# Moving the eight weight sums of the last batch from VectorE to GpSimd

## The chip, the cores and the metric

The program runs on one core of one Trainium2 chip. A core has five engines with a queue of instructions each: TensorE (PE, with its weight loads shown as PEld), VectorE (DVE), ScalarE (ACT), GpSimd (POOL) and SyncE (SP, which here issues the DMAs of inputs, outputs and transposes). An engine takes its instructions in the order in which they stand in its queue; a semaphore holds an instruction until what it needs is there. The metric is the device time of one execution in microseconds. The number of a kernel is the median of its runs.

## The reference

Two layers follow each other, with four batches of 768 rows, 8 heads of 64 columns, 512 columns in all. The first is a recurrent attention with a decay for each head; the second mixes the rows and columns by a Fourier transform, normalizes, and puts two matrix products with a ReLU between them on top:

```python
for t in range(S):
    state = gamma * state + einsum(k[:, :, t], v[:, :, t])
    y[:, :, t] = scale * einsum(q[:, :, t], state)
x = y with the heads side by side                 # 4 x 768 x 512
u = x + real(fft(fft(x, axis=1), axis=2))
un = (u - mean(u)) / sqrt(var(u) + 1e-06)         # per row
out = u + maximum(un @ w_ch1, 0.0) @ w_ch2        # w_ch1 512 x 2048, w_ch2 2048 x 512
```

## The kernel before, in words

**Stages.** Each batch goes through the same stages. The heads come in pairs, four pairs to a batch. `cast_unit` (L417) turns a pair's q, k and v into f16 on GpSimd. `t_unit` has q and k transposed. `a_unit` (L657) makes the products of queries and keys on TensorE in three parts, and VectorE multiplies each part by a mask into the tile `atm` (L668). `kv_unit` (L674) makes the running states. `y_unit` (L700) adds up a pair's output on TensorE, from the states (L715) and from `atm` (L719), and ScalarE writes it to `x` (L727). `fold_s` (L744), `fold_d` (L771) and `fold_e` (L785, L787) add and subtract halves of `x` on VectorE, all in f16 with both inputs in SBUF, which shortens the Fourier products that follow (`s1_unit` L848, `s2_unit` L1010). `s2_unit` ends with two additions of `x` on GpSimd (L1038, L1040). `norm_unit` makes the statistics (L1050, L1051) and the normalized rows `un` (L1052), which are transposed into `unT`. Then come the two products of the channel layer.

**The channel layer.** In the first three batches `h_unit` (L1088, evicted by ScalarE L1092 or VectorE L1094) makes the hidden rows and `ch_unit` (L1127, L1131) the output rows. In the last batch, number 3, the second product goes through a seven-product scheme for 2 x 2 blocks. The rows come in three groups of 256. For each group `hp_unit` (L1175) makes the hidden blocks, evicted by ScalarE (L1180) and in one half by VectorE (L1183), VectorE adds some of them up (L1193), and `p_unit` (L1217) makes the seven products; VectorE adds each to where it belongs (L1222). Four of the products have sums of blocks of the second weight `w216` on their right side. These are the tiles `wsum`. `wsum_unit` (L1152) makes them: for k of 1 to 4 and for two parts, one subtraction of 128 x 1024 f16 elements each, so eight instructions. The sums for k = 2 and k = 4 take the sums for k = 1 and k = 2 as their second input. The eight tiles come from the pool `inp`, of 11 buffers, which also holds the loaded q, k and v.

**The order of the work.** The function `tile_retnet_recurrent__then__fnet_fourier_mix_kernel` collects units of work in streams. A stream has a first and a last due time, in units of one batch, and its units are spread evenly between them. `emit` (L1373) sorts all units by due time; that gives the order in the program. The framework then puts each engine's instructions in the order of its queue: by the order in the program, but with what is ready ahead of what isn't, as its own estimate of durations has it, so an instruction can come out well ahead of its due time. Two helpers tie the order down: `pin`, for the first batch, and `held` (L148), which adds to every instruction of a unit an order-only edge to the instruction just ahead of it in the program on the same engine. `cast_unit` is `held` that way.

**Around the change.** The last `cast_unit` of batch 3 is due at about 2.30. The stream of `wsum_unit` runs from `b + WS[0]` to `b + WS[1]` with b = 3, so from 3.00 to 3.12, beside the first units of the last batch's channel layer, and it isn't `held`. The next instructions of GpSimd in the program after the last cast are those of `s2_unit` for batch 3, the first of them due at about 2.73.

Of the kernel before, what the change touches and what calls it, by code (L numbers as in the profile page):

```python
# [53 lines left out]
LD0, LD1 = (0.223, 0.312), (-0.370, 0.140)  # L54
HT0 = (0.666, 0.693, 0.632, 0.590)
NPE = 2
WS = (0.0, 0.12)
KD = (2, 3)
NT = 0.6
ACT_ROWS = ((2, 5, 6, 7, 8, 9, 10, 14), (0, 3, 6, 7, 9, 10, 11, 12, 14, 15))  # L60
# [3 lines left out]
def kernel(  # L64
# [9 lines left out]
    nc = tc.nc  # L74
# [29 lines left out]
    w216 = const.tile([P, NFB, DM], f16, tag="w216")  # L104
# [43 lines left out]
    def held(unit):  # L148
        def run():
            ins = tc.nc.cur_bb.bb.instructions  # L150
            n0 = len(ins)
            unit()
            for n in range(n0, len(ins)):
                m = n - 1
                while m >= 0 and ins[m].engine != ins[n].engine:
                    m -= 1
                if m >= 0:
                    tc.add_manual_dep(ins[n], ins[m].name,
                                      mybir.DependencyInfo(mybir.DependencyClass.NoSync,
                                                           mybir.DependencyReason.DATA),  # L160
                                      reason="casts in turn")
        return run
# [232 lines left out]
    for j in range(2):  # L395
# [6 lines left out]
        t = const.tile([P, 257], f32, tag=f"qn_{j}", name=f"qn_{j}", padded_shape=[P, 260])  # L402
# [463 lines left out]
    def g0_unit(b, parts=(0, 1, 2)):  # L866
        def run():
            for part in parts:
                (g0_a, g0_b, g0_c)[part](b)
        return run  # L870
# [185 lines left out]
    def rstd_unit(b, rt):  # L1056
        def run():
            stats = lb[b]["st"]
            if b == 0 and rt == 0:
                bn_unit(0)()  # L1060
            sl = slice(3 * rt, 3 * rt + 3)
            nc.scalar.activation(stats[:, sl, 2:3], stats[:, sl, 1:2], AF.Sqrt, bias=epsT,
                                 scale=1.0)
            nc.vector.reciprocal(out=stats[:, sl, 3:4], in_=stats[:, sl, 2:3])
        return run

    def unT_unit(b, kb):
        def run():
            un, unT = lb[b].pop(("un", kb)), lb[b]["unT"]
            if b > 1 or b and kb >= 3:  # L1070
                nc.sync.dma_start_transpose(unT[:, :, kb * P:(kb + 1) * P], un)
                return
            pst = ps_g.tile([P, 4, P], f16, tag="g", name="pst", padded_shape=[P, 8, P])
            for cb in range(4):
                nc.tensor.transpose(pst[:, cb, :], un[:, cb * P:(cb + 1) * P], ident16)
            if (kb % 2 == 0) != (b == 0 and kb < 3):
                nc.vector.tensor_copy(unT[:, :, kb * P:(kb + 1) * P], pst)
            else:
                nc.scalar.copy(unT[:, :, kb * P:(kb + 1) * P], pst)
        return run  # L1080
# [61 lines left out]
    def spare(n, name):  # L1142
        return flat(inp.tile([P, 2, NCH, D], f32, tag="in32", name=name))[:, 0:n]
# [5 lines left out]
    def half_of(w, fh, eh, n0, n1):  # L1149
        return w[:, 8 * fh + n0:8 * fh + n1, 256 * eh:256 * eh + 256]  # L1150

    def wsum_unit(k, part):  # L1152


        def run():
            n0, n1 = 4 * part, 4 * part + 4
            t = seven["t", k, part] = spare(4 * 256, "wsum").rearrange("p (n m) -> p n m", n=4)
            a, b = {1: ((0, 1), (0, 0)), 2: ((1, 1), None), 3: ((1, 1), (0, 1)),
                    4: ((1, 0), None)}[k]
            in1 = half_of(w216, *b, n0, n1) if b else seven["t", k // 2, part]  # L1160
            nc.vector.tensor_tensor(out=t, in0=half_of(w216, *a, n0, n1), in1=in1,
                                    op=ALU.subtract)
        return run

    def hp_unit(b, g, n):

        def run():
            unT = lb[b]["unT"]
            if (g, n) == (0, 0):
                seven["s4"] = spare(8 * P, "s4").rearrange("p (n k) -> p n k", n=8)  # L1170
            psh = ps_pm.tile([P, 2, 256], f32, tag="pm", name="psh")
            for t in range(2):
                fb = n + 8 * t
                for cb in range(4):
                    nc.tensor.matmul(psh[:, t], w116[:, cb, fb * P:(fb + 1) * P],  # L1175
                                     unT[:, cb, g * 256:(g + 1) * 256],
                                     start=(cb == 0), stop=(cb == 3))
            for t0, t1, eng in (((0, 1, "a"), (1, 2, "v")) if n == 7 else ((0, 2, "a"),)):
                if eng == "a":
                    nc.scalar.activation(hg[:, n, t0:t1], psh[:, t0:t1], AF.Relu, bias=0.0,  # L1180
                                         scale=-1.0)
                else:
                    nc.vector.tensor_scalar(out=hg[:, n, t0:t1], in0=psh[:, t0:t1], scalar1=-1.0,  # L1183
                                            scalar2=0.0, op0=ALU.mult, op1=ALU.max)
            if n in (2, 5, 7):
                sl = slice({2: 0, 5: 3, 7: 6}[n], n + 1)
                a11, a12 = hg[:, sl, 0, 0:P], hg[:, sl, 1, 0:P]
                a21, a22 = hg[:, sl, 0, P:256], hg[:, sl, 1, P:256]
                s1, s2, s4 = sg[:, 0, sl], sg[:, 1, sl], seven["s4"][:, sl]
                for out_, x, y, op in ((s1, a21, a22, ALU.add), (s2, s1, a11, ALU.subtract),  # L1190
                                       (s4, a12, s2, ALU.subtract),
                                       (a21, a11, a21, ALU.subtract)):
                    nc.vector.tensor_tensor(out=out_, in0=x, in1=y, op=op)  # L1193
        return run
# [198 lines left out]
    streams = []  # L1393
    for b in range(B):
        majors = []
        if b == B - 1:
            for g in range(3):
                majors += [hp_unit(b, g, n) for n in range(8)]
                if g < 2:
                    majors.append(rstd_unit(b, g))  # L1400
                majors += [p_unit(b, g, k) for k in (1, 4, 5, 6, 2, 7, 3)]
            streams.append(([wsum_unit(k, part) for part in range(2) for k in (1, 2, 3, 4)],
                            b + WS[0], b + WS[1]))
        elif b == 0:
            for kb in range(3):
                if kb:
                    majors.append(unT_unit(0, kb))
                majors += [h0_unit(kb, g) for g in range(4)]
        else:
            majors += [h_unit(b, 0, fb) for fb in range(NFB)]  # L1410
        if b < B - 1:
            majors.append(rstd_unit(b, 0))
            majors += [ch_unit(b, 0, rb3, part) for rb3 in range(3) for part in range(4)]
            majors += [h_unit(b, 1, fb) for fb in range(NFB)]
            majors.append(rstd_unit(b, 1))
            majors += [ch_unit(b, 1, rb3, part) for rb3 in range(3) for part in range(4)]
        streams.append((majors, b, b + 1.0))
        streams += mix_units(b, [3, 4, 5], *(b + t for t in (DM0 if b == 0 else DM1)))
        if b + 1 < B:
            steps = attn_steps(b + 1)  # L1420
            if b == 0:
                streams.append(([load_unit(1, i, 6) for i in range(4)], LD0[0], LD0[1]))
                streams.append(([qt_zeros], 0.1, 0.15))
                streams.append(([half_tables], HT0[0], HT0[1]))
                streams.append(([pad_unit], HT0[2], HT0[3]))
                ts = TS0
            else:
                streams.append(([load_unit(b + 1, i) for i in range(4)], b + LD1[0], b + LD1[1]))
                n = [len(u) for u in steps[1:]]
                ts = list(TS1[:2]) + [TS1[2] + TS1[3] * sum(n[:j]) / sum(n) for j in range(6)]  # L1430
            streams.append((steps[0], b + ts[0], b + ts[1]))
            streams += [(u, b + ts[j + 2], b + ts[j + 3]) for j, u in enumerate(steps[1:])]
            end = b + ts[-1]
            da = DA0 if b == 0 else DA1
            sums = [s1_unit(b + 1, e, cb) for cb in range(2) for e in range(2)]
            sums.insert(1, g0_unit(b + 1, (1, 2)))
            streams.append((sums, end + da[0], end + da[1]))
            streams += mix_units(b + 1, [0, 1, 2], *(end + t for t in da[2:]))
# [31 lines left out]
```

## Time and profile before

| | |
|---|---|
| median of 3 runs | 242.05 us (241.75 to 242.3) |
| the profiled execution | 243.38 us, of which the span of its instructions is 240.6 us |
| granted TensorE clock | 0.999 |
| busy in the span | PE 226.1 us, DVE 189.6 us, ACT 125.2 us, POOL 82.0 us |
| the eight sums (L1161, DVE) | starts at 139.0, 140.4, 158.7, 159.5, 200.1, 201.1, 202.7 and 203.5 us |
| last batch's channel layer | first matmul at 194.63 us, last at about 237 us |

Times in the profile are microseconds from the span's start. A row of the time line gives the start, the duration from the first start to the last end of a run of like instructions, the engine, the line, the operation, output and inputs, shapes, and how many there are (x2: two, merged in one row); in square brackets stands how long the engine sat idle before it and what ended the wait. A row of a source line gives the least, the median and the greatest duration in ns. A row of a stretch gives its length and each engine's busy time in it. The chain of work that ended last is followed back from the last instruction, at each step to what released it.

### The profile page before, as it was taken

How to read it: one execution, taken by the hardware profiler on the slowest of the kernel's cores; microseconds unless marked ns; L12 is line 12 of the kernel's file. 1: busy time of each engine (PE TensorE's matmuls, PEld its weight loads, DVE VectorE, ACT ScalarE, POOL GpSimd, SP SyncE). 2: the span in 40 equal slices, each digit the busy share in tenths (PEclk: the TensorE clock that was granted, in tenths of full speed). 3: DMA queues.
4: the chain of work that ended last, by engine and by line, in shares of the span. 5: the costliest groups of instructions: out<-in, count | busy, mean ns of one | idle time of the engine just before them, and what ended most of it. 6: DMA issues, size and time to landing. Idle time of an engine off the chain costs nothing.

```text
span 240.6 us, 5573 instructions
## 1 busy us (share of the span) xinstructions
PE 226.1 (94%) x2127; PEld 154.8 (64%) x2127; DVE 189.6 (79%) x472; ACT 125.2 (52%) x272; POOL 82.0 (34%) x148
## 2 busy tenths in 40 slices
PE   0888999999999999999899999999999998899994
PEld 0366779756774656665567446655675477688883
DVE  8699987948898889977886759997886529968473
ACT  5989759675864544931147405822356336251430
POOL 7378802575300197850001817930003204200000
PEclk9999999999999999999999999999999999999999
DMA  7999999999999489979999587675100240140202
GB/s 169 236 269 260 207 207 207 217 245 247 243 232 213 78 193 217 186 142 123 256 277 210 112 177 203 131 120 159 44 3 0 70 131 0 40 115 1 90 0 87
DMA packets 101241, 36.78 MB, mean 153 GB/s; under 512 B 91488, under 2 KB 98528, under 8 KB 101216
## 3 DMA queue, kind: packets, MB, share of 16 engines
q1 hardware_dynamic: 96992, 32.25, 63.5%
q0 software_dynamic: 4224, 4.19, 10.6%
q8 instruction: 16, 0.26, 0.5%
q14 instruction: 9, 0.07, 0.1%
HBM read 27.26 MB, written 6.29 MB: 139 GB/s over the span
## 4 chain that ended last, share of the span: by engine, by line
PE 79%; DVE 7%; DMA 6%; POOL 2%; ACT 2%; issue 1%; SPq 1%; POOLq 0%; DVEq 0%
PE psc L1127 23%; PE psh L1088 21%; PE ps L1217 7%; PE psh L1175 6%; PE psh L1105 3%; PE wkA L665 3%; DMA qTz<-q16z 3%; DMA v<-in_v_dram 3%; PE ps L848 3%; PE wkY L719 2%; PE pq L1010 1%; PE ps L828 1%; PE wkY L715 1%; PE wkK L684 1%; SPq L217 1%
## 5 line engine op out<-in xcount | busy, mean ns | idle before, releaser
L1127 PE MATMUL psc<-w,ht 128*128 128x512 f16 x288 | 67.7, 379 | 0.0
L1088 PE MATMUL psh<-unT,w 128*128 128x384 f16 x320 | 59.5, 326 | 0.0
L1038 POOL TENSOR_TENSOR u<-u,x 128x256 f32<-128x256 f32 x21 | 13.8, 655 | 109.7 <-DVE u L1017 97.4
L1127 PEld LDWEIGHTS <-ht 128*128 128x128 f16 x288 | 27.2, 98 | 26.5
L1088 PEld LDWEIGHTS <-w 128*128 128x128 f16 x320 | 29.9, 98 | 15.9 <-DMA unT<-un 0.4
L1092 ACT ACTIVATE ht<-psh 128x384 f16<-128x384 f32 x46 | 22.3, 489 | 24.1 <-PE psh L1088 23.6
L668 DVE TENSOR_TENSOR atm<-wkA,maskp 128x512 f16<-128x512 f32 x36 | 23.6, 682 | 2.1 <-PE wkA L665 2.1
L1180 ACT ACTIVATE ht<-psh 128x512 f16<-128x512 f32 (+1 forms) x24 | 13.6, 569 | 19.3 <-PE psh L1175 17.1
L1052 ACT ACTIVATE un<-u,stats 128x512 f16<-128x512 f32 x21 | 14.7, 718 | 15.5 <-DVE stats L1051 9.0
L1175 PE MATMUL psh<-unT,w 128*128 128x256 f16 x192 | 22.6, 273 | 0.0
L1131 DVE SCALAR_TENSOR_TENSOR ob<-psc,stats,u 128x512 f32<-128x512 f32 x18 | 13.4, 744 | 9.9 <-PE psc L1127 9.7
L1094 DVE TENSOR_SCALAR ht<-psh 128x384 f16<-128x384 f32 x34 | 18.7, 550 | 2.7 <-PE psh L1088 2.5
L1175 PEld LDWEIGHTS <-w 128*128 128x128 f16 x192 | 18.6, 98 | 2.5 <-DMA unT<-un 0.2
L694 DVE SCALAR_TENSOR_TENSOR s<-s,gk,wkK 128x128 f16<-128x128 f16 x48 | 16.2, 337 | 2.3 <-ACT s L690 1.6
L727 ACT ACTIVATE x<-wkY,gexp 128x384 f16<-128x384 f32 x24 | 12.9, 580 | 9.0 <-PE wkY L719 8.9
L1050 DVE BATCH_NORM_STATS2 bst<-u 128x6 f32<-128x512 f32 x21 | 14.4, 687 | 3.2 <-POOL u L1040 2.8
L1217 PEld LDWEIGHTS <-ht 128*128 128x128 f16 x144 | 13.8, 98 | 4.1 <-ACT ht L1180 1.5
L439 POOL TENSOR_SCALAR kd<-k,gexp 128x384 f16<-128x384 f32 x24 | 13.8, 585 | 3.7 <-DMA k<-in_k_dram 3.6
L1193 DVE TENSOR_TENSOR ht<-ht 128x384 f16<-128x384 f16 (+1 forms) x27 | 9.2, 369 | 6.1 <-ACT ht L1180 5.9
L665 PE MATMUL wkA<-qTz,kT 128*128 128x256 f16 x72 | 13.2, 272 | 0.6 <-DMA qTz<-q16z 0.6
L1040 POOL TENSOR_TENSOR u<-u,x 128x256 f32<-128x256 f32 x21 | 13.4, 640 | 1.0 <-DVE u L1020 1.0
L1217 PE MATMUL ps<-wsum,ht 128*128 128x256 f16 x96 | 12.1, 273 | 0.4 <-DVE ht L1183 0.4
(190 smaller groups left out, 396.3 us busy)
## 6 DMA issues: line engine op xcount, KB each, us to landing
q<-in_q_dram SPq DMA_DIRECT2D x16, 384.0 KB, 5.9
k<-in_k_dram SPq DMA_DIRECT2D x16, 384.0 KB, 5.6
v<-in_v_dram SPq DMA_DIRECT2D x16, 384.0 KB, 5.9
out_dram<-ob SPq DMA_DIRECT2D x21, 256.0 KB, 2.7
w<-in_moe_w_ch_dram POOLq DMA_DIRECT2D x8, 512.0 KB, 10.7
out_dram<-ob SPq DMA_DIRECT2D x5, 128.0 KB, 2.0
unT<-un SPq DMA_TRANSPOSE x15, 2.5
kT<-kd SPq DMA_TRANSPOSE x10, 3.0
```

What stands on the lines that cost most here:

```text
L439: kc = nc.gpsimd.tensor_scalar(out=kd[:, :, h2, :], in0=k32[:, h2], scalar1=gkd[:, h0 + h2:h0 + h2 + 1], scalar2=1.0, op0=ALU.mult, op1=AL ...
L665: mm = nc.tensor.matmul(wk[:, c2], st["kT"][:, c, :], st["qT"][:, :, c, :], start=True, stop=True)
L668: nc.vector.tensor_tensor(out=st["atm"][:, 2 * part:2 * part + 2], in0=wk, in1=maskp[:, PAIR_ORDER[i]].unsqueeze(1).to_broadcast([P, 2, 2, ...
L694: nc.vector.scalar_tensor_tensor(out=s16[:, c], in0=s16[:, c - 1], scalar=gk2[:, hp:hp + 1], in1=wk[:, c - c0], op0=ALU.mult, op1=ALU.add)
L1050: nc.vector.bn_stats(bst, u[:, kb, :])
L1052: nc.scalar.activation(un, u[:, kb, :], AF.Identity, bias=stats[:, kb, 0:1], scale=-1.0)
L1088: nc.tensor.matmul(psh, w116[:, cb, fb * P:(fb + 1) * P], unT[:, cb, rt * 384:(rt + 1) * 384], start=(cb == 0), stop=(cb == 3))
L1092: nc.scalar.activation(ht16[:, fb, :], psh, AF.Relu, bias=0.0, scale=-1.0)
L1094: nc.vector.tensor_scalar(out=ht16[:, fb, :], in0=psh, scalar1=-1.0, scalar2=0.0, op0=ALU.mult, op1=ALU.max)
L1127: nc.tensor.matmul(psc, ht16[:, fb, rb3 * P:(rb3 + 1) * P], w216[:, fb, :], start=(fb == 0), stop=(fb == NFB - 1))
L1175: nc.tensor.matmul(psh[:, t], w116[:, cb, fb * P:(fb + 1) * P], unT[:, cb, g * 256:(g + 1) * 256], start=(cb == 0), stop=(cb == 3))
L1217: nc.tensor.matmul(ps[:, c0:c1], lhsT, rhs[:, c0:c1], start=bool(new and n == 0), stop=(n == 7), skip_group_check=True)
```

## The change

The eight subtractions of `wsum_unit` are issued on GpSimd in place of VectorE. Their due times go from 3.00 to 3.12 down to 2.42 to 2.60, behind the last casts of q, k and v, and each is `held`, so that GpSimd takes them in turn behind the last cast. What is subtracted from what, the tiles and their pool stay.

```diff
-WS = (0.0, 0.12)
+WS = (-0.58, -0.40)
...
             in1 = half_of(w216, *b, n0, n1) if b else seven["t", k // 2, part]
-            nc.vector.tensor_tensor(out=t, in0=half_of(w216, *a, n0, n1), in1=in1,
+            nc.gpsimd.tensor_tensor(out=t, in0=half_of(w216, *a, n0, n1), in1=in1,
                                     op=ALU.subtract)
...
-            streams.append(([wsum_unit(k, part) for part in range(2) for k in (1, 2, 3, 4)],
+            streams.append(([held(wsum_unit(k, part)) for part in range(2) for k in (1, 2, 3, 4)],
                             b + WS[0], b + WS[1]))
```

## The prediction

> **What bounds the kernel now.** I read first the busy time by stretch, to see where TensorE isn't full, then the chain that ended last for those places, then the time line of GpSimd and VectorE where the sums would go.
>
> ```profile
> 158.50:167.00 8.50, 8.50 (x86) 4.99 (x84) 6.95 (x16) 2.31 (x5) 0.01 (x1) 1.00 0.69 124
> 167.00:179.00 12.00, 12.00 (x103) 7.60 (x101) 11.12 (x25) 4.30 (x10) 0.00 (x0) 1.00 0.12 45
> 194.60:212.80 18.20, 16.54 (x154) 13.99 (x153) 15.11 (x38) 8.72 (x20) 4.28 (x6) 1.00 0.17 40
> 212.80:223.70 10.90, 10.90 (x102) 9.75 (x100) 8.11 (x22) 3.44 (x7) 0.00 (x0) 1.00 0.16 56
> ```
>
> The columns are the stretch, its length, and busy PE, PEld, DVE, ACT and POOL. TensorE is the bound: it is full in every row but the third, the last batch's first group, where it lacks 18.20 - 16.54 = 1.66 us. That is all that the change can win there. The second row is the one to remember: there VectorE is 11.12 of 12.00 us busy and TensorE has no gap either.
>
> ```profile
> 200.20 0.60 DVE wsum L1161
> 201.20 0.60 DVE wsum L1161
> 202.19 0.60 DVE bst L1050
> 203.54 0.58 DVE wsum L1161
> PE ps L1217 <- ACT ht L1180: 1.2, 1, 1.2
> PE ps L1217 <- DVE ht L1183: 0.4, 1, 0.4
> ```
>
> The chain runs through three of the sums (four rows of the chain, then two of the waits between 194 and 214 us). The statistics that they hold up hold up ScalarE, which comes late with the last hidden block; hence the 1.2 and 0.4 us in which TensorE waits.
>
> **What the change takes from VectorE.** Eight sums, of which four stand outside that group:
>
> ```profile
> 139.04 0.77 DVE L1161 TENSOR_TENSOR wsum<-w 128x1024 f16<-128x1024 f16 x1
> 143.13 0.75 DVE L1131 SCALAR_TENSOR_TENSOR ob<-psc,stats,u 128x512 f32<-128x512 f32 x1 [2.06 <-PE psc L1127]
> 158.68 0.66 DVE L1161 TENSOR_TENSOR wsum<-w 128x1024 f16<-128x1024 f16 x1
> 161.16 0.75 DVE L1131 SCALAR_TENSOR_TENSOR ob<-psc,stats,u 128x512 f32<-128x512 f32 x1 [0.32 <-PE psc L1127]
> ```
>
> The two near 139 us are followed by 2.06 us in which VectorE has nothing to do, the two near 159 us by 0.32 us, and TensorE is full there: nothing is won. The four in the first group take some 0.6 us each, 2.4 us of VectorE. Bounds: 1.66 us won if every wait of TensorE there goes, and half a microsecond lost if the new order of VectorE's queue happens to be worse. I take 1.4 won, since the two waits are near the sums (1.2 + 0.4) and small ones remain.
>
> **What it puts on GpSimd.** The time from the last cast to GpSimd's next work, and durations from which to price a sum:
>
> ```profile
> 157.67 0.83 POOL L444 TENSOR_SCALAR v<-v 128x768 f16<-128x768 f32 x1
> 183.25 0.63 POOL L1038 TENSOR_TENSOR u<-u,x 128x256 f32<-128x256 f32 x1 [24.74 <-DVE u L1017]
> L1038 POOL TENSOR_TENSOR u<-u,x x21: 632/635/1016, 40.4 to 204.9; 128x256 f32<-128x256 f32 x21
> L480 POOL TENSOR_SCALAR v<-v 128x768 f16<-128x768 f32 x2 | 1.7, 830 | 5.1 <-DMA v<-in_v_dram 5.1
> L480 POOL TENSOR_SCALAR v<-v 128x384 f16<-128x384 f32 x3 | 1.5, 501 | 0.5 <-DMA v<-in_v_dram 0.5
> ```
>
> The sums can start at 158.5, when the last cast ends. A cast of one input costs (830 - 501) / 384 = 0.857 ns an element and 0.17 us beside that. The two-input addition of 256 elements takes 0.635 us. With the same 0.17 us fixed, it costs 1.81 ns an element, and 1024 elements take 2.03 us. With nothing fixed they take four times 0.635, 2.54 us; with the rate of a cast and all the rest fixed, 1.29 us. I take 2.2 us, between the first two, since that row is the same operation. The Trainium skill (GPSIMD Engine Reference, section 3.1) gives 4497 ns for 2048 f32 elements; a line through that and our 635 ns gives an estimate of 2.29 us, by which the sum below would be some 0.6 us more. Eight sums are 17.6 us, to 176.1: well ahead of 183.25, where GpSimd's next work would queue behind them, and ahead of the products that need them (from 203 us). No DMA is issued or moved. Seen alone, that is free.
>
> **What they collide with.** VectorE's and GpSimd's instructions get in each other's way if VectorE's has two inputs in SBUF:
>
> ```profile
> 198.10 0.63 POOL L1038 TENSOR_TENSOR u<-u,x 128x256 f32<-128x256 f32 x1 [10.02 <-DVE u L1017]
> 198.69 0.75 POOL L1040 TENSOR_TENSOR u<-u,x 128x256 f32<-128x256 f32 x1
> 198.33 0.62 DVE L1193 TENSOR_TENSOR ht<-ht 128x384 f16<-128x384 f16 x1
> 198.33 1.33 DVE L1193 TENSOR_TENSOR ht<-ht 128x384 f16<-128x384 f16 x2
> L1193 DVE TENSOR_TENSOR s<-ht x9: 284/346/353, 199.9 to 233.1; 128x384 f16<-128x384 f16 x6, 128x256 f16<-128x256 f16 x3
> 17.24 1.17 POOL L368 TENSOR_SCALAR ssn<-ssp 128x1158 f16<-128x1158 f16 x1
> 17.81 0.80 DVE L761 TENSOR_TENSOR xab<-x 128x387 f16<-128x387 f16 x1
> L668 DVE TENSOR_TENSOR atm<-wkA,maskp x36: 656/681/692, 56.3 to 171.1; 128x512 f16<-128x512 f32 x36
> ```
>
> An L1193 addition takes 0.35 us alone. The one that starts at 198.33 under a GpSimd addition ends at 198.95, just behind GpSimd's end at 198.73. The next ends at 199.66, behind the end of the second GpSimd addition (199.44), which had come in between. So each waits for the whole instruction of the other, and they go in turn. The longest hold in this trace is at 17.24: an L761 that would take 0.35 us takes 0.80, until GpSimd's 1.17 us are over. An instruction with one input in PSUM doesn't wait: L668 keeps to 656 to 692 ns, casts beside it or not. No run yet shows a hold of 2.2 us. The Trainium skill (SBUF — State Buffer, "SBUF: two separate sides") says that the pair of ports which VectorE and GpSimd share is locked for the whole instruction, whatever its length; by that rule the price is the one below, and the trace agrees as far as its 1.17 us reach.
>
> Now what VectorE has to do while the sums run:
>
> ```profile
> 167.10 1.04 DVE L744 TENSOR_TENSOR xab<-x 128x780 f16<-128x780 f16 x2 [0.16 <-ACT x L727]
> 168.17 1.03 DVE L771 TENSOR_TENSOR eo<-xab 128x768 f16<-128x768 f16 x2
> 169.12 0.68 DVE L668 TENSOR_TENSOR atm<-wkA,maskp 128x512 f16<-128x512 f32 x1
> 170.53 1.28 DVE L668 TENSOR_TENSOR atm<-wkA,maskp 128x512 f16<-128x512 f32 x2
> 173.43 1.01 DVE L744 TENSOR_TENSOR xab<-x 128x768 f16<-128x768 f16 x2
> 171.69 0.59 PE L719 MATMUL wkY<-v,atm 128*128 128x64 f16 x12
> 172.11 6.10 PE L1088 MATMUL psh<-unT,w 128*128 128x384 f16 x36
> ```
>
> At 167.10 VectorE begins four folds in a row, L744 twice and L771 twice, all f16 with both inputs in SBUF. Sum 4 ends at 158.5 + 4 x 2.2 = 167.3, so the first fold waits 0.2 us. Sum 5 then goes ahead of the second fold, sum 6 ahead of the third, sum 7 ahead of the fourth: 3 x 2.2 = 6.6 us. VectorE is through at 169.1 + 6.8 = 175.9. Behind it in its queue stand the three L668 that make `atm`, and TensorE's L719 needs all three. Before, the last ends at 170.53 + 1.28 = 171.81 and L719 begins at 171.69: no slack. TensorE's queue is in order, so the 36 matmuls of L1088 wait behind L719: **TensorE stands for 6.8 us.** The last sum ends near 177.7, before the next pair of folds (173.43 + 6.8 = 180.2), so nothing more is held up. Bounds for a sum of 2.03 to 2.54 us: 6.8 to 8 us or so, by where in a sum the first fold falls; for 1.29 us, where seven are over when it arrives, some 1.7 us.
>
> **What the standing costs beyond itself.** Matmuls after a long idle time, and the same shape in mid-run:
>
> ```profile
> 5.61 0.82 PE L497 MATMUL tq<-ident,q16z 128*128 128x128 f16 x6 [5.61 <-POOL q16z L454]
> 8.13 1.91 PE L172 MATMUL wps<-ht 128*128 128x512 f16 x4
> 10.81 1.21 PE L172 MATMUL wps<-ht 128*128 128x512 f16 x3
> 164.48 1.03 PE L1127 MATMUL psc<-w,ht 128*128 128x512 f16 x4
> ```
>
> After 5.61 us idle at the program's start, four matmuls of 512 columns take 1.91 us, against 1.03 later: half the speed, though the granted clock is shown as full there. Three at 10.81 take 1.21 us, between 0.81 at full and 1.48 at half speed, so the speed came back near 11.4, some 3.3 us after the dense work began. If 6.8 us of standing have the same effect, TensorE loses half of 3.3 us: 1.7 us. Bounds: 0, since it may be a matter of the start alone, and 1.9 (half of the 3.8 us from 8.13 to the first full-speed work near 11.95). I take 1.7, as the idle times are alike. The Trainium skill (TensorE: Matmul & The Clock Gate, Part 1) says that an idle window of about 3.4 us halves the clock until about 3.4 us of sustained work; by that the price is 1.7 us as well, and no run here shows an idle time of that length in mid-run.
>
> **The sum**, against the profiled execution: 6.8 + 1.7 - 1.4 = 7.1 us on a span of 240.6 and a time of 243.38, so 250.5 for that one. The median of the runs is 242.05, 1.33 less; from it the prediction is 242.05 + 7.1 = **249.1 us**.
>
> **The rivals.** *The clock holds.* All as above without the 1.7: 247.4 us. For it: no mid-run case in the trace.
>
> *Short sums.* If GpSimd takes f16 faster, say 1.5 us a sum, five are over by 166.0 and the sixth ends at 167.5. The first fold waits 0.4, the next two 1.5 each: 3.4 - 1.4 = 2.0, so 244.0 us, with a standing too short to slow the clock. Against it: GpSimd's f16 instruction at 17.24 costs 1.17 us for 1158 elements, the rate of its f32 casts.
>
> *No collision, the change does what it says.* It wins its 1.4 us: 240.7 us, faster. It decides if the sums are over before the first fold, which takes under 8.6 / 8 = 1.08 us a sum, or if the folds come elsewhere in VectorE's new queue. Against it: the row of 0.635 us for a quarter of the elements, and that the folds at 167.10 start when ScalarE's L727 lets them, whatever the sums do.
>
> *GpSimd goes first each time.* If its next sum takes the ports before a waiting fold does, the first fold waits for all eight: 176.1 - 167.1 = 9.0, and 9.0 + 1.7 - 1.4 = 9.3, so 251.4 us. The turns at 198 us speak against it.
>
> **How the numbers follow.** Chances: forecast 0.46, the clock holds 0.20, short sums 0.12, GpSimd first 0.08, no collision 0.11, no change to be told 0.03. No change is within 0.2%, about what a measurement of this kernel can tell. The first four are slower: 0.86. The forecast alone lies in 248 to 251 us; the range from the short sums to GpSimd first, 243.6 to 251.6 us, leaves out 0.14.
>
> **What would show it.** In the changed profile, eight GpSimd subtractions from 158.5 on, near 2.2 us each, four of them longer by a few tenths; the folds L744 and L771 that follow them over 2 us each in place of 0.55; TensorE waiting for VectorE's L668 at L719 by some 7 us; then matmuls of 384 columns at twice their spacing for about 3 us; and between the start of the last channel layer and its second group nearly no wait of TensorE. It is wrong if the folds keep their 0.55 us under a running sum, if the sums are through by 167, or if the framework places the four folds or the sums elsewhere.

## The result, and the profile after

The changed kernel takes 250.11 us (median of 4 runs, 249.79 to 251.55). The kernel before, run beside it on the same chip, takes 242.18 us (4 runs, 241.75 to 243.01). The ratio is 1.0335, with a 95% interval of 1.0286 to 1.0384: slower by 3.4%, 7.9 us. The profiled execution took 250.03 us, its span is 248.3 us against 240.6, and its mean granted clock is 0.986.

The page's busy times of the changed kernel, and below them five stretches of it (columns as in the prediction: the stretch, its length, busy PE, PEld, DVE, ACT and POOL, granted clock, and what the DMA engines did):

```profile
PE 227.7 (92%) x2127; PEld 155.6 (63%) x2127; DVE 192.2 (77%) x464; ACT 125.4 (50%) x272; POOL 99.3 (40%) x156
```

```profile
167.00:179.00 12.00, 5.26 (x47) 3.21 (x45) 11.90 (x9) 0.64 (x2) 8.52 (x4) 0.81 0.08 29
202.60:220.80 18.20, 16.77 (x156) 14.30 (x155) 13.21 (x35) 8.80 (x20) 3.80 (x6) 1.00 0.19 51
...
174.00:175.00 1.00, 0.00 (x0) 0.00 (x0) 1.00 (x1) 0.00 (x0) 1.00 (x1) 0.70 0.00 0
175.00:176.00 1.00, 0.00 (x0) 0.00 (x0) 1.00 (x2) 0.00 (x0) 0.60 (x1) 0.50 0.00 0
181.00:182.00 1.00, 1.00 (x7) 0.53 (x5) 0.95 (x3) 0.43 (x1) 0.00 (x0) 0.88 0.00 0
```

The stretch from 167 to 179 us had TensorE busy for all of its 12.00 us; now it is busy for 5.26. VectorE looks as busy as ever (11.90 in place of 11.12), but with 9 instructions in place of 25: a blocked instruction counts as busy. That is why the busy share of the whole run doesn't show the trouble: VectorE's total went up by 2.6 us although eight instructions were taken from it. The last three rows are the granted clock around the standstill.

The time line of the same place in the changed kernel, for POOL, DVE and PE (start, duration, engine, line, what, and the idle time ahead of it):

```profile
157.84 2.13 POOL L1161 TENSOR_TENSOR wsum<-w 128x1024 f16<-128x1024 f16 x1
...
166.29 2.12 POOL L1161 TENSOR_TENSOR wsum<-w 128x1024 f16<-128x1024 f16 x1
168.49 2.33 POOL L1161 TENSOR_TENSOR wsum<-w,wsum 128x1024 f16<-128x1024 f16 x1
170.78 2.43 POOL L1161 TENSOR_TENSOR wsum<-w 128x1024 f16<-128x1024 f16 x1
173.17 2.42 POOL L1161 TENSOR_TENSOR wsum<-w,wsum 128x1024 f16<-128x1024 f16 x1
```

```profile
166.47 2.37 DVE L744 TENSOR_TENSOR xab<-x 128x780 f16<-128x780 f16 x1 [0.16 <-ACT x L727]
168.76 2.48 DVE L744 TENSOR_TENSOR xab<-x 128x780 f16<-128x780 f16 x1
171.27 2.35 DVE L771 TENSOR_TENSOR eo<-xab 128x768 f16<-128x768 f16 x1
173.55 2.47 DVE L771 TENSOR_TENSOR eo<-xab 128x768 f16<-128x768 f16 x1
175.94 0.68 DVE L668 TENSOR_TENSOR atm<-wkA,maskp 128x512 f16<-128x512 f32 x1
```

```profile
176.67 0.29 PE L719 MATMUL wkY<-v,atm 128*128 128x64 f16 x2 [5.46 <-DVE atm L668]
177.93 0.29 PE L719 MATMUL wkY<-v,atm 128*128 128x64 f16 x2 [0.97 <-DVE atm L668]
178.53 0.61 PE L719 MATMUL wkY<-v,atm 128*128 128x64 f16 x8 [0.31 <-DVE atm L668]
178.95 7.23 PE L1088 MATMUL psh<-unT,w 128*128 128x384 f16 x36
```

Read the first two fences against each other. Sum 5 begins at 166.29 and ends at 168.41; the fold that begins at 166.47 ends at 168.84. Sum 6 begins at 168.49, the second fold ends at 171.24, behind sum 6's end at 170.82. So they go on in turns, four sums and four folds, and the sums too are a little longer now (2.33 to 2.43 us against 2.13). The four pairs take 9.47 us, from 166.47 to 175.94, so 2.37 us a pair. That is less than a sum alone (one begins every 2.09 us) and a fold alone (0.52) would take one behind the other, 2.61: a sum costs the fold that meets it 1.86 us, not its whole length. Why they overlap by that much, no run here shows. L668, which needs no turn, keeps its 0.68 us but starts at 175.94; the first one after the folds started at 169.12 before. TensorE has the waits in brackets of the third fence, 5.46 + 0.97 + 0.31 = 6.74 us, and then the 36 matmuls that took 6.10 us take 7.23.

Then the last batch's first group. First two rows of ScalarE in the kernel before, then the waits of TensorE in the changed kernel (total, times, longest), and three rows of its ScalarE there:

```profile
203.63 0.72 ACT L1052 ACTIVATE un<-u,stats 128x512 f16<-128x512 f32 x1 [1.40 <-DVE stats L1051]
204.26 0.36 ACT L1180 ACTIVATE ht<-psh 128x256 f16<-128x256 f32 x1
```

```profile
PE wkY L719 <- DVE atm L668: 6.7, 3, 5.5
PE ps L1217 <- ACT ht L1180: 1.3, 2, 1.0
```

```profile
209.81 0.72 ACT L1052 ACTIVATE un<-u,stats 128x512 f16<-128x512 f32 x1 [0.71 <-DVE stats L1051]
211.62 0.72 ACT L1052 ACTIVATE un<-u,stats 128x512 f16<-128x512 f32 x1 [0.28 <-issue]
212.25 0.36 ACT L1180 ACTIVATE ht<-psh 128x256 f16<-128x256 f32 x1
```

The statistics do come earlier without the sums on VectorE. Before, one normalization (L1052) that waits for them stood in ScalarE's queue ahead of its last eviction of a hidden block (L1180). Now there is one ahead of each of the last two evictions, and TensorE waits for those by 1.3 us, where it waited 1.2 + 0.4 us before.

Where the 7.7 us of the span come from, by when the same instruction starts in the two traces: the first L665 of the last pair starts 0.64 us earlier than before (167.94 against 168.58), in work that the change doesn't touch: TensorE waited 0.2 us less at the program's start and 0.45 us less for a transpose near 116 us. That is spread between executions and no gain: in the traces of the twelve kernels below, three of them with all sums on VectorE, the same instruction starts between 167.63 and 168.46 us. From there to the 36 matmuls of L1088 7.48 us are lost (178.95 - 172.11 = 6.84, and the 0.64); the 36 matmuls cost 1.13 more, which puts the next stage (the first L848) 7.96 us late; the last channel layer's first L1175 is still 7.96 late, and that of its third group 7.75. So the first group gave back 0.21 us.

### The profile page after: what moved, and what is told of

It is laid out like the page before. It is cut to its first block, busy times and chain, and to the rows that moved or that the text cites. A ratio compares the mean times of both kernels' runs of the same rounds, so it can differ in the third digit from the quotient of the medians.

```text
span 248.3 us, 5572 instructions
## 1 busy us (share of the span) xinstructions
PE 227.7 (92%) x2127; PEld 155.6 (63%) x2127; DVE 192.2 (77%) x464; ACT 125.4 (50%) x272; POOL 99.3 (40%) x156
## 4 chain that ended last, share of the span: by engine, by line
PE 75%; DVE 11%; DMA 6%; POOL 2%; issue 2%; ACT 2%; SPq 1%; DVEq 0%
PE psc L1127 20%; PE psh L1088 20%; PE psh L1175 6%; PE ps L1217 6%; PE psh L1105 3%; DMA v<-in_v_dram 3%; PE wkA L665 3%; DMA qTz<-q16z 3%; PE ps L848 3%; DVE xab L744 2%; PE wkY L719 2%; PE pq L1010 1%; PE ps L828 1%; DVE eo L771 1%; PE wkK L684 1%
## 5 line engine op out<-in xcount | busy, mean ns | idle before, releaser
L1088 PE MATMUL psh<-unT,w 128*128 128x384 f16 x320 | 60.6, 330 | 0.0
L1038 POOL TENSOR_TENSOR u<-u,x 128x256 f32<-128x256 f32 x21 | 13.3, 635 | 100.6 <-DVE u L1017 88.3
L1088 PEld LDWEIGHTS <-w 128*128 128x128 f16 x320 | 30.3, 99 | 16.6 <-issue 1.5
L668 DVE TENSOR_TENSOR atm<-wkA,maskp 128x512 f16<-128x512 f32 x36 | 23.6, 683 | 1.6 <-PE wkA L665 1.6
L1180 ACT ACTIVATE ht<-psh 128x512 f16<-128x512 f32 (+1 forms) x24 | 13.7, 570 | 20.3 <-PE psh L1175 20.3
L1175 PE MATMUL psh<-unT,w 128*128 128x256 f16 x192 | 22.3, 272 | 0.0
L1052 ACT ACTIVATE un<-u,stats 128x512 f16<-128x512 f32 x21 | 14.9, 719 | 14.2 <-DVE stats L1051 8.3
L1175 PEld LDWEIGHTS <-w 128*128 128x128 f16 x192 | 18.7, 98 | 2.3
L1193 DVE TENSOR_TENSOR ht<-ht 128x384 f16<-128x384 f16 (+1 forms) x27 | 8.8, 353 | 8.3 <-ACT ht L1180 8.0
L719 PE MATMUL wkY<-v,atm 128*128 128x64 f16 x144 | 7.6, 197 | 6.7 <-DVE atm L668 6.7
L1040 POOL TENSOR_TENSOR u<-u,x 128x256 f32<-128x256 f32 x21 | 13.4, 640 | 0.0
L665 PE MATMUL wkA<-qTz,kT 128*128 128x256 f16 x72 | 13.2, 272 | 0.2 <-DMA qTz<-q16z 0.2
```

What stands on the lines that cost most here:

```text
L665: mm = nc.tensor.matmul(wk[:, c2], st["kT"][:, c, :], st["qT"][:, :, c, :], start=True, stop=True)
L668: nc.vector.tensor_tensor(out=st["atm"][:, 2 * part:2 * part + 2], in0=wk, in1=maskp[:, PAIR_ORDER[i]].unsqueeze(1).to_broadcast([P, 2, 2, ...
L1052: nc.scalar.activation(un, u[:, kb, :], AF.Identity, bias=stats[:, kb, 0:1], scale=-1.0)
L1088: nc.tensor.matmul(psh, w116[:, cb, fb * P:(fb + 1) * P], unT[:, cb, rt * 384:(rt + 1) * 384], start=(cb == 0), stop=(cb == 3))
```

## The experiments

The theory: GpSimd's sums hold VectorE's additions of two SBUF operands, instruction by instruction, and the standstill of TensorE is that hold passed on through the queue. A first rival: the framework's new order of VectorE's queue is what comes late whatever GpSimd does. A second: GpSimd's being busy is enough, by whatever it does.

**Half the sums behind the casts.** Four sums stay where the change put them and so are over before the folds; the other four go to a gap of GpSimd near 188 us.

```diff
-            streams.append(([held(wsum_unit(k, part)) ...], b + WS[0], b + WS[1]))
+            sums = [held(wsum_unit(k, part)) for part in range(2) for k in (1, 2, 3, 4)]
+            streams.append((sums[:4], b + WS[0], b + WS[1]))
+            streams.append((sums[4:], b - 0.20, b - 0.12))
```

> Four of the sums stay behind the last casts, the other four go to GpSimd's idle time after the last batch's first three additions (from about 188 us). Lock theory: the fourth sum ends about 166.2 us, before the first fold at 166.5, so the four folds keep their 0.55 us each, TensorE doesn't wait at L719 beyond 0.1 us and its clock stays at 1.00; what is left is the first group of the last channel layer as the changed kernel had it, 0.2 us better than before: about 242.0 us, within 0.2% of the kernel before or just faster. Rival (the framework's new queue order costs the time, not the lock): near 250 us, since the order of VectorE's queue is nearly that of the changed kernel.

241.75 us (12 runs), ratio to the kernel before 0.998, interval 0.9959 to 1.0001. Of its time line the fourth sum on POOL and the folds on DVE, and the stretch from 167 us:

```profile
164.73 2.11 POOL L1161 TENSOR_TENSOR wsum<-w,wsum 128x1024 f16<-128x1024 f16 x1
```

```profile
166.98 1.04 DVE L744 TENSOR_TENSOR xab<-x 128x780 f16<-128x780 f16 x2 [0.15 <-ACT x L727]
```

```profile
167.00:179.00 12.00, 12.00 (x103) 7.67 (x102) 11.22 (x25) 4.36 (x9) 0.00 (x0) 1.00 0.12 45
```

The fourth sum ends at 166.84, 0.14 us ahead of the first fold; the folds are back at 0.5 us each and TensorE is full again. Eight sums on GpSimd are not the trouble, four of them beside the folds are. The rival of VectorE's queue order falls: from the folds to the third L668 the order of VectorE's queue is the same in all three kernels.

**The same time on GpSimd, without reading.** The eight sums are left out and their tiles written twice by memsets instead, so GpSimd is busy from 157.9 to 173.2 us.

```diff
-            nc.gpsimd.tensor_tensor(out=t, in0=half_of(w216, *a, n0, n1), in1=in1,
-                                    op=ALU.subtract)
+            for _ in range(2):
+                nc.gpsimd.memset(t, 0.0)
```

> Every sum is replaced by two memsets of its tile (1024 f16 elements each) in the same place of GpSimd's queue, so the sums are left out and the tiles hold zeros; GpSimd is busy for about the same 16 us and writes SBUF, but reads nothing. Theory (what VectorE waits for is the shared read port): the four folds keep 0.55 us and the time is about 242 us. Rival (any GpSimd instruction holds the folds up): folds of 1.5 us or more each, a time of 246 us or more.

241.55 us, one run. POOL and DVE of that time line:

```profile
157.92 15.27 POOL L1162 MEMSET wsum<- 128x1024 f16 x16
```

```profile
166.57 1.04 DVE L744 TENSOR_TENSOR xab<-x 128x780 f16<-128x780 f16 x2 [0.15 <-ACT x L727]
```

A memset takes 15.27 / 16 = 0.95 us, and with turns of that length each fold would have grown by most of a memset. The folds don't grow at all: two take 1.04 us. So the second rival falls too: being busy on GpSimd, and writing the same tiles, isn't enough. What the memsets lack is the sums' reading of SBUF. The Trainium skill (SBUF — State Buffer, "SBUF: two separate sides") says that a VectorE instruction with two SBUF inputs contends with a GpSimd instruction that reads SBUF, and not with one that only writes it; this pair of runs agrees (0.52 us beside memsets, 2.35 to 2.48 beside subtractions).

**One and two holds.** Five and six sums behind the casts in place of four, so that one and two folds meet a sum.

```diff
-            streams.append((sums[:4], b + WS[0], b + WS[1]))
-            streams.append((sums[4:], b - 0.20, b - 0.12))
+            streams.append((sums[:5], b + WS[0], b + WS[1]))
+            streams.append((sums[5:], b - 0.20, b - 0.12))
```

> Five of the sums behind the last casts, three late. Lock theory: the fifth runs from about 166.3 to 168.4 us, so the first fold takes about 2.4 us and the other three 0.55; VectorE is 1.8 us late, of which 0.7 us is slack (7.5 us late gave 6.7 us of waiting in the changed kernel), so TensorE waits about 1.1 us at L719, clock 1.00, about 243.1 us. Rival (the queue order): near 250 us.

> Six of the sums behind the last casts, two late. Lock theory: two folds of about 2.4 us, VectorE 3.75 us late, TensorE waits about 3.0 us at L719, less than the 3.3 us after which the clock fell in the changed kernel, so clock 1.00 and about 245.1 us. If the clock falls all the same, 1 us more. Rival (GpSimd keeps the ports while it has sums in its queue): the first fold takes over 4 us and the second 0.55.

243.41 and 245.42 us, one run each, 0.3 us over what was expected. Of the time lines of DVE, the first row is of the kernel with five, the second of that with six:

```profile
166.66 2.84 DVE L744 TENSOR_TENSOR xab<-x 128x780 f16<-128x780 f16 x2 [0.15 <-ACT x L727]
```

```profile
166.86 4.77 DVE L744 TENSOR_TENSOR xab<-x 128x780 f16<-128x780 f16 x2 [0.15 <-ACT x L727]
```

Two folds in 1.04, 2.84 and 4.77 us: one hold more costs 1.8 to 1.9 us. TensorE's waits at L719 are 0, 1.4, 3.1 and, with four holds, 6.7 us; the spans are 240.2, 241.6, 243.7 and 248.3. Of holds of 1.8, 3.7 and, in the changed kernel, 7.45 us in all, 1.4, 3.1 and 6.7 us reach TensorE as waits; 0.4 to 0.7 us are covered. With four holds the span grows by 8.1 us, 1.4 more than the waits: for the most part the clock, next.

**The clock by itself.** The changed kernel with 34 matmuls that do nothing useful ahead of the last pair's L715, to keep TensorE at work through the first part of the standstill. All that the kernel computes is still computed.

```diff
+            if (b, i) == (B - 1, 3):
+                for n in range(34):
+                    nc.tensor.matmul(yk[0].rearrange("p c d -> p (c d)"), w116[:, 0, 0:P],
+                                     w116[:, 1, 0:384], start=True, stop=True)
```

> The changed kernel, with 34 matmuls of 384 columns (about 5.5 us of work at full clock, whose result is overwritten) put ahead of the last pair's L715, so that TensorE is busy while VectorE waits. Theory (the standing halved TensorE's clock from 174.4 to 181.2 us, which cost 1.1 us on the 36 matmuls behind): the granted clock stays 1.00, the 36 matmuls take 6.1 us in place of 7.2, the wait at L719 is 1 us or less, and the time is about 249.0 us, 1.1 under the changed kernel. Rival (the matmuls are slow for another reason, such as late evictions): no gain.

248.83 us, ratio to the kernel before 1.0269, interval 1.0224 to 1.0315. In its time line of PE (lines lie 4 further on):

```profile
170.64 5.69 PE L710 MATMUL wkY<-w 128*128 128x384 f16 x34
...
178.67 6.10 PE L1092 MATMUL psh<-unT,w 128*128 128x384 f16 x36
```

The 36 matmuls are at 6.10 us again, the mean granted clock is 1.000, and they start at nearly the same time (178.67 against 178.95). So the halved clock cost some 250.11 - 248.83 = 1.3 us of the changed kernel's time (an estimate from the medians of four runs each), and the rest is the standstill itself. TensorE still waited 1.4 us for `atm`, a little more than expected. The rival in which the clock holds falls.

**The sums on GpSimd at their old due times.** Against the kernel before, the engine is changed and the sums are `held`; against the changed kernel it is one line.

```diff
-WS = (-0.58, -0.40)
+WS = (0.0, 0.12)
```

> The sums on GpSimd with the due times of the kernel before (3.00 to 3.12), one part of the change undone. Lock theory: no sum runs beside the folds L744 and L771, so no wait at L719. But only three sums fit before the additions at 198 us; three follow at about 200 to 206 and two at 207 to 211, beside L1193, which has two inputs in SBUF and waits for them, and the products need the eighth sum at about 207 us: TensorE waits 3 to 6 us in the first group, about 246 us.

250.66 us, one run. The folds are back at 1.04 us for two, as expected; but the time is 4.7 us worse than expected, since the sums come both late for the products that need them and in the way of the hidden blocks' additions. The time line of VectorE, the waits of TensorE, and two slices of a microsecond with the granted clock:

```profile
197.72 3.54 DVE L1193 TENSOR_TENSOR ht<-ht 128x384 f16<-128x384 f16 x3
201.18 2.27 DVE L1193 TENSOR_TENSOR s<-ht 128x384 f16<-128x384 f16 x1
```

```profile
PE ps L1217 <- ACT ht L1180: 4.2, 1, 4.2
PE ps L1217 <- POOL wsum L1161: 3.1, 1, 3.1
```

```profile
206.00:207.00 1.00, 0.32 (x2) 0.15 (x3) 1.00 (x3) 0.90 (x3) 1.00 (x3) 0.66 0.00 0
212.00:213.00 1.00, 1.00 (x6) 0.48 (x4) 0.54 (x1) 0.00 (x0) 0.43 (x1) 0.50 0.00 0
```

An L1193 of 0.35 us takes 2.27 here: the same hold, in another place. With another 0.4 us for VectorE's half block, TensorE waits 7.7 us in the group. The clock fell here as well, from about 206.3 to 216.6 us; TensorE was busy for some 6.4 us of that at half speed, which makes some 3.2 us of loss (an estimate from the slices) that the expectation did not have. Moving the sums ahead was no mistake in itself; they had to stop before the folds.

**Where the gain in the first group went.** With the holds gone (four and four) the time still isn't told from that of before, with TensorE waiting 1.3 us for ScalarE, as in the changed kernel. A first theory: only ScalarE's order is wrong. So blocks 3 to 5 of the last batch are normalized behind ScalarE's last eviction of a hidden block (`behind_act` adds an order-only edge to the instruction just ahead on ScalarE); once on the kernel with four and four, once on the kernel before.

```diff
+        if (b, kbs[0]) == (B - 1, 3):
+            return [([s2_unit(b, kb) for kb in kbs], s0, s1),
+                    ([behind_act(norm_unit(b, kb)) for kb in kbs], b + 0.1703, b + 0.1712),
+                    ([unT_unit(b, kb) for kb in kbs], u0, u1)]
```

> As e_four, and ScalarE's three normalizations L1052 of the last batch's second half are put behind the eviction of the last hidden block of the first group. Theory (the 1.3 us that TensorE still waited in the first group are ScalarE's, which stood in L1052 for statistics ahead of that eviction): the wait falls below 0.4 us, and the time is about 241 us, 1 us under e_four. Rival (VectorE's remaining work is the limit there): no more than 0.3 us under e_four.

> The kernel before with all sums on VectorE, and ScalarE's normalizations put behind the eviction as in e_four_act. Theory (ScalarE's order alone made the wait of 1.2 us, the sums only lengthened it): about 241.2 us, 0.8 us faster than before. Rival (the sums on VectorE are what is late, since they stand ahead of the additions of hidden blocks and of the statistics): 241.8 to 242.4, within 0.2% of before.

243.51 us (ratio 1.0043, 1.0015 to 1.007) and 246.17 us (1.017, 1.0127 to 1.0213). The waits of TensorE in the first of them (lines lie 17 further on):

```profile
PE ps L1234 <- DVE ht L1200: 1.8, 1, 1.8
PE ps L1234 <- DVE ht L1210: 0.4, 1, 0.4
```

The wait for ScalarE is gone, and one for VectorE's half of the last hidden block (L1183 in the unchanged numbering) has come in its place, since the statistics still stand ahead of that. The theory falls. In the kernel before, the same edit makes TensorE wait 2.0 us for transposed rows as well. These waits are not the whole of the two times. In the trace of the second the granted clock is at 0.50 from about 210.3 to 213.7 us, right behind the waits. The trace of the first is of an execution of 242.02 us without such a fall in its middle (mean granted clock 0.997), but five of its twelve runs had 0.991 and spans of 242.0 to 242.5 us, where the other seven had 240.2 to 241.1; what fell in those five no trace shows. Next block 5's Fourier products, statistics and normalization become due later, among the group's products:

```diff
-            return [([s2_unit(b, kb) for kb in kbs], s0, s1),
-                    ([behind_act(norm_unit(b, kb)) for kb in kbs], b + 0.1703, b + 0.1712),
+            return [([s2_unit(b, 3), s2_unit(b, 4)], s0, b + 0.093),
+                    ([behind_act(norm_unit(b, 3)), behind_act(norm_unit(b, 4))], b + 0.1703, b + 0.1712),
+                    ([s2_unit(b, 5)], b + 0.235, b + 0.235),
+                    ([norm_unit(b, 5)], b + 0.25, b + 0.25),
```

> As e_four (four sums behind the casts, four from 188 us, all on GpSimd), and the last batch's second half is put behind the first group's hidden blocks on two engines: ScalarE's normalizations of row blocks 3 and 4 behind the eviction of the last hidden block, and row block 5's Fourier products and statistics due between the first products, so that neither ScalarE nor VectorE has them ahead of that eviction. Theory (TensorE's 1.3 us in e_four and 2.2 us in e_four_act are one and the same shortage: statistics and normalizations ahead of the last hidden block, on whichever engine they stand): TensorE waits less than 0.5 us in the first group, and the time is about 240.9 us, 0.8 under e_four and 0.5% faster than before. Rival (another late piece takes its place, such as the additions L1193 or the transposes of the second group): within 0.3 us of e_four, 241.5 to 242.1.

> The reordering of e_best alone, with the sums on VectorE as in the kernel before. Theory (the reordering makes the gain possible, but the four sums in the first group, 2.4 us of VectorE, stand ahead of the additions L1193 and of the last eviction): TensorE still waits about 1 us, so about 241.8 us, 0.9 us over e_best. Rival (the order alone was the trouble, the sums hide): within 0.3 us of e_best.

242.09 us (0.9989, 0.9968 to 1.0011) with four and four, 243.28 us (1.0034, 1.0013 to 1.0054) with the sums on VectorE. With four and four TensorE waits 1.0 us for the output rows' additions (L1222) and 0.9 for VectorE's half block, so the rival holds: once more another piece is late. With the sums on VectorE it waits 2.3 us, where about 1 was expected. At last block 4's statistics and normalization go behind the additions of the last hidden block (`behind_adds`, an order-only edge on VectorE to the last L1193), and block 5, with the transposes, later by about a tenth of a batch:

```diff
-                    ([behind_act(norm_unit(b, 3)), behind_act(norm_unit(b, 4))], b + 0.1703, b + 0.1712),
-                    ([s2_unit(b, 5)], b + 0.235, b + 0.235),
-                    ([norm_unit(b, 5)], b + 0.25, b + 0.25),
+                    ([behind_act(norm_unit(b, 3)), behind_act(behind_adds(norm_unit(b, 4)))], b + 0.1703, b + 0.1712),
+                    ([s2_unit(b, 5)], b + 0.345, b + 0.345),
+                    ([norm_unit(b, 5)], b + 0.365, b + 0.365),
-                    ([unT_unit(b, kb) for kb in kbs], u0, u1)]
+                    ([unT_unit(b, 3), unT_unit(b, 4)], b + 0.232, b + 0.305), ([unT_unit(b, 5)], b + 0.40, b + 0.40)]
```

> Four sums on GpSimd as in the run with four, and in the last batch's first group the normalization of block 3 is put behind ScalarE's last eviction of a hidden block, that of block 4 and its statistics behind VectorE's additions of the last hidden block, and block 5's statistics and transposes later by about one second-matrix block. If the 1.3 us of TensorE waiting in that group come only from pieces that stand ahead of the last hidden blocks' evictions on ScalarE and VectorE, the waits of TensorE at the second product fall to under 0.5 us and the time to about 240.9 us (0.8 under the run with four). If the group has no slack for the moved pieces, another one (transposes that come late, or statistics ahead of an addition) takes the place of the wait and the time stays between 241.5 and 242.5 us.

> The kernel before, all eight sums on VectorE at their old due times, with the same reordering of the last batch's first group as in the run at 240.76 us; nothing else. If the sums' place is worth what it was with the first reordering (1.2 us), VectorE's sums delay the statistics or the additions, TensorE waits for VectorE in that group by about 2 us instead of 0.8, and the time is near 241.9 us. If the reordering alone made the gain, and the sums' place adds nothing, the waits stay under 1 us and the time is near 240.8 us.

With four and four: **240.76 us** (12 runs), ratio to the kernel before 0.994, interval 0.9916 to 0.9965. With the sums on VectorE as in the kernel before: 242.56 us, 1.0014, 0.9994 to 1.0034. The stretch of the first group and the waits of TensorE there (lines lie 30 further on), first with four and four, then with the sums on VectorE:

```profile
194.60:212.80 18.20, 17.66 (x167) 15.56 (x166) 13.40 (x34) 8.97 (x20) 5.09 (x7) 1.00 0.19 60
```

```profile
PE ps L1247 <- DVE u L1252: 0.5, 1, 0.5
PE psh L1205 <- ACT ht L1210: 0.3, 1, 0.3
```

```profile
194.60:212.80 18.20, 16.19 (x152) 13.91 (x150) 15.58 (x38) 7.96 (x18) 4.62 (x6) 1.00 0.13 31
```

```profile
PE ps L1247 <- DVE ht L1213: 1.1, 1, 1.1
PE psh L1205 <- DMA unT<-un: 0.5, 1, 0.5
PE ps L1247 <- DVE wsum L1191: 0.4, 1, 0.4
```

TensorE lacks 0.54 us of the stretch, against 1.66 in the kernel before (the group begins 0.8 us earlier in this trace, and the wait of 0.3 falls just behind the stretch). With the sums on VectorE and the same order it lacks 2.01, and VectorE is 2.2 us busier. So the sums' place is worth 242.56 - 240.76 = 1.8 us in this order, and 243.28 - 242.09 = 1.2 us in the one before it; neither the move of four and four nor the order alone makes the kernel faster by anything that can be told. This kernel beats both the kernel before and the changed one. The gain in the group itself is smaller than the times say: from its first L1175 to that of the third group it takes 28.14 us in place of 29.07, 0.9 us less, and the medians of the spans are 239.05 against 240.0 for the kernel before beside it, and 240.35 with the sums on VectorE. What is left of the differences lies outside the span. The waits left (0.8 us) were a little more than expected (under 0.5); the time was as expected. With the sums on VectorE the waits were the 2 us expected, and the time was 0.7 us more.

## Why the prediction was right

It gave 249.1 us, in a range of 243.6 to 251.6, and slower with 0.86. Step by step:

- **The price of a sum**, 2.2 us from the rows of L1038 and the casts: measured 2.13, one begun every 2.1 us. The estimate of 2.29 from the f32 figure of the Trainium skill (GPSIMD Engine Reference, section 3.1) was a little further off.
- **The hold**, instruction by instruction and in turns, from pairs of 0.6 to 1.2 us: it goes on to 2.1 us, and in turns. Shown by the folds, by the kernels with four, five and six, and by the memsets that don't hold. The size of a hold was taken as a whole sum, 2.2 us, and is 1.8 to 1.9.
- **The standstill**, 6.8 us forecast: 6.74 us of waits, but 7.48 us lost between L665 and L1088. VectorE's four folds took 9.47 us in place of 2.02, 7.45 more. The first fold was to wait 0.2 us for sum 4; it met sum 5, 0.18 us after that had begun, because the sums were begun every 2.1 us and not every 2.2, so that four were over just before the fold came. So four sums went between, not three. With a sum begun every 2.09 us the prediction's own rule gives 1.9 + 3 x 2.09, some 8.1 us, and at its bound of 2.54 us a sum 1.6 + 3 x 2.54 = 9.2, above the 8 that it gives. What was measured is less because each of the four holds cost 1.86 us. So one hold too few and holds too long nearly cancelled: that the waits came out at 6.74 against 6.8 is luck. Of the 0.74 us beside the waits, 0.6 are the twelve L719 that go in three pieces at the lower clock (1.19 us in place of 0.59).
- **The clock**, 1.7 us forecast from the program's start: 1.13 us in the 36 matmuls, 1.3 us in the comparison with the filled standstill. The mechanism is right, and the size too large by 0.4 us: at full speed again after some 2.7 us of dense work, not 3.3. That the size came so near is partly chance, since the time to full speed is no fixed amount of dense work. At the program's start, from which it was taken, the three matmuls of L172 take 0.82 us in the changed kernel's trace (full speed by 10.61 us, at most 2.7 us after the first L172) and 1.46 us, half speed throughout, in four of the others; in the trace with the memsets the ten matmuls behind them still take 0.74 us in place of 0.47, which puts the return some 4.6 us after the first L172 (an estimate).
- **The gain in the first group**, 1.4 us forecast: 0.2 us. This is the step that was mis-sized. That "the two waits are near the sums" was right, but the sums weren't the only thing ahead of the last hidden blocks. With the statistics early, a normalization came ahead of each of the last two evictions on ScalarE, and the wait stayed at 1.3 us. It took an order by hand, on two engines, to have some 0.9 us of it.

The terms as measured are 7.5 + 1.1 - 0.2 - 0.6 (the last in the work ahead of the change) = 7.8, against the 7.7 us by which the two profiled spans differ. The 0.6 is chance between two executions: without it the terms make 8.4, and the median span of the changed kernel's four runs, 248.4 us, lies 8.5 above the 239.9 of the kernel before (23 runs beside the experiments). Against the forecast's 7.1 the standstill cost 0.7 more, the clock 0.6 less, and the first group gave 1.2 less, 1.3 us in all. The medians of the times, which lie 7.9 apart, make it 0.8. The profiled times differ by 6.65 us only, because that of before lay 1.2 us above its median.

Of the rivals, the held clock falls by the granted clock in the profile, short sums by their 2.13 us, no collision and GpSimd first by the turns. (In the forecast's case of 1.29 us a sum, six sums are over when the first fold comes and the seventh runs; the 1.7 us given for it are right.) Without the folds the price would have been about none, as four and four shows.

## What to carry to other kernels

Before work is given to GpSimd, look at what VectorE does in every stretch in which it would run. An addition of two SBUF tiles that meets a GpSimd instruction which reads SBUF waits until it is over, in turns, and what is queued behind waits too; if TensorE waits for that, the price is nearly the number of such meetings times GpSimd's duration (here 1.8 to 1.9 us for a sum of 2.1), and the clock on top. Split the moved work so that it ends before such a stretch. And when a late piece is taken out of a crowded stretch, ask which piece comes late next: here it took three reorderings until the time moved.

## What the runs showed of the hardware that had not been expected

The granted clock fell in mid-run and the profile shows it there: the last matmul before the standstill ended at 171.2 us, the column goes to 0.70 in the slice from 174 to 175 us (it changes near 174.4, some 3.2 us on), stays at 0.50 and is 0.88 from 181 to 182 (it changes near 181.2, 2.7 us after dense work began at 178.5). With the sums on GpSimd at their old due times it fell about 3.8 us after the last matmul (202.5 to 206.3 us). The Trainium skill (TensorE: Matmul & The Clock Gate, Part 1) gives an idle window of about 3.4 us; these two traces agree.

A wait of that length isn't needed for a fall, though. In the kernel before with ScalarE's normalizations put behind the eviction, the clock fell near 210.3 us, where TensorE had worked for some 1.2 of the 3.4 us ahead of that and its longest wait was 2.0 us. In the kernel with six sums, 3.1 us of waits in pieces of at most 1.7 us left it at 1.00. The three halved stretches of these traces last 6.8 us (174.4 to 181.2), 10.2 us (206.3 to 216.6) and 3.4 us (210.3 to 213.7): two, three and one times 3.4 us. So in these traces the halved clock comes in steps of that length, and what it costs depends on how much TensorE has to do in them.

At the program's start the same column had shown full speed while matmuls took twice their time. It says nothing there: the clock's record in the changed kernel's trace begins only near 10.6 us, just where the matmuls of L172 are at full speed.

A GpSimd memset of 128 x 1024 f16 takes 0.95 us and leaves VectorE's two-input additions at 0.52 us each, though it writes to SBUF all the while. Where VectorE's additions and GpSimd's subtractions do take turns, a pair takes 2.37 us, 0.24 less than the two would one behind the other.
